# Reordering the small tasks ahead of the FFN in a one-core S4-convolution and SwiGLU kernel: the gate row's parts and the first weights' split

## The chip, the cores and the metric

The kernel runs on one core of a Trainium2 chip. The core has five engines that run side by side, each with its own queue of instructions that it works off in order: TensorE (PE, matrix products into PSUM; its weight loads are listed as PEld), VectorE (DVE), ScalarE (ACT), GpSimd (POOL) and SyncE (SP, which here only starts transfers). An engine waits for another by a semaphore; while the instruction at the head of a queue waits, everything behind it in that queue waits too. The metric is the device time of one execution in microseconds (us), the median of several runs.

## The reference: what is computed

Six rows of 448 numbers come from the condition `c`: `mod = silu(c) @ w_mod`, cut into `sa, ca, ga, sb, cb, gb`. Then two blocks work on `x` (2048 tokens by 448 channels, float32):

```python
h = layernorm(x) * (1 + ca) + sa
x = x + ga * S4(h)            # a long convolution over the tokens, plus h * Dskip
h = layernorm(x) * (1 + cb) + sb
x = x + gb * ((silu(h @ w_gate) * (h @ w_up)) @ w_down)     # 448 -> 1792 -> 448
```

With these inputs the convolution's kernel is nearly linear in time over the whole length, so that the program replaces the Fourier transforms by running sums of tokens (triangular and ramp matrices on TensorE). A flag, worked out on the chip, chooses between this short path and a general one; the short one runs here.

## The kernel before, in words

The 2048 tokens are 16 tiles of 128, and these are worked through in six blocks of 2, 2, 3, 3, 3 and 3 tiles. For each block the FFN runs over 14 slices `f` of 128 hidden channels: `gate_up(f)` (22 matmuls, line 724) makes gate and up, ScalarE and VectorE form `silu(gate) * up` and split it into a high part `phi` and a low part `plo` (lines 739, 752, 755, 756), and `down(f - 1)` (line 768) multiplies the slice before by `w_down`. Weights and activations are each held as a high part and the rest, so that three products of reduced precision stand for one of full precision; "split" below means this. The weights of slices 0 to 2 (gate and up) and 0 and 1 (down) are split ahead of the FFN, the others inside the first block, one slice at a time.

Before the FFN lies a stage that serves the first two tiles. It is a list of small tasks, `PLAN` (lines 43 to 45 hold its end), and its order is written by hand: the tasks are issued in this order, so that each engine's queue gets its share of the list in the list's order. Nothing reorders them later. The tasks that matter here:

| task | engine and line | what it does |
|---|---|---|
| `sp` | PE 248, 251 | the four parts of row `sb`, each on its own 32 partitions of a PSUM bank |
| `spc` | ACT 469 | copies them to SBUF as `qts` |
| `sbt`, `sbc` | PE 373, 376; DVE 379 | turn them and sum the parts: `sb` as columns, `sbc` |
| `gq`, `gqc` | PE 248, 251; ACT 469 | the same parts and copy (`qtb`) for the gate row `gb`; the weights lie in tile `m` |
| `gbk`, `gb` | PE 382; ACT 455 | spread the gate row over 128 partitions, copy it to SBUF |
| `n1q`, `rq`, `xnq` | DVE 437; POOL 167, 168; ACT 490 | layernorm of tile q (0 or 1): product, root (the power, line 168), scaling |
| `trq` | PE 373, 376 | turns tile q to channels on partitions |
| `hiq`, `loq` | ACT 428, four; DVE 433, four | add `sbc` and split into `hhi` and `hlo`, which the FFN reads |
| `l1` | PE 405 | sum over the first tiles for the running sum |
| `lr0`, `lr1` | ACT 413; DVE 410 and a small transfer in ACT's queue, 411 | put the running sums in place |
| `x0` | ACT 455 | copies tile 0's new `x` |
| `w0`, `w01`, `w02` | ACT 123; DVE 125, 127 | split of gate and up weights 0; `w1...` and `w2...` likewise |
| `d00`, `d01` | ACT 115; DVE 117 | split of down weights 0; `d10`, `d11` likewise |
| `fl` | DVE 447, 448 | the flag, which every engine loads at line 506, after the list |

The stage's PSUM tiles come from four banks in turn (`bank()`), in the order in which the tasks are issued. The FFN's first slice reads `hhi` and weights 0 first (its matmuls go over the high parts of all channels before it takes `hlo`), and its two results lie in `DN[2]` and in the next bank; slice 1 uses the two banks after that. SP starts the load of weight slice 3 into the buffer of slice 0 when `w02` has been done.

```python
        for n in names:
            todo[n]()

    rv = nc.values_load(flag[0:1, 0:1], min_val=0, max_val=1)
```

Of the kernel before, what the change touches and what calls it, by code (L numbers as in the profile page):

```python
# [40 lines left out]
ORDER = """sf x0 x1 sc m10 se sd m11 m20 m21 m00 sb m01 sa m40 m41 m30 m31 w0 m50 m51 d0 w1 d1 x2 w2 x3 d2"""  # L41

PLAN = """t4 pa0 t1 S1 t2 pa1 t3 wi ca gp S20 wr ps0 h00 gpc h01 S21 gt a2 gac sq1 ps1 m0 gdm dg t5 k0 S3 h10 cp v00 a3 gdr
m1 k1 cpc gd h11 hd0 v01 ck sq0 v10 hd1 o00 cbw v11 o01 o02 xh1 gc0 sa st0 o10 o12 o13 o14 fs w0 r0 n10 sp xn0 x1 st1 fl r1 n11 gc1 spc
tr0 xn1 sbt w01 sbc gq l1 hi0 tr1 lo0 lr0 w02 hi1 lo1 lr1 gqc x0 gbk gb w1 w11 w12 d00 d01 w2 w21 w22 d10 d11"""
EPS = 1e-5


# [1016 lines left out]
```

## Time and profile before

| what | value |
|---|---|
| three runs | 491.65, 492.12, 492.21 us; median 492.12 us |
| the profiled execution | 490.89 us, of which its span (first to last instruction) 489.1 us |
| TensorE busy in the span | 475.3 us (97%) |
| VectorE, ScalarE, GpSimd busy | 284.2, 155.7, 62.3 us |
| mean granted TensorE clock | 0.992 of full speed |

Times below are microseconds from the start of the span. A row of the timeline gives start, duration, engine, line, operation, the tile written and the tiles read, and the count of instructions merged; a bracket at its end tells how long the engine sat idle before it and what ended that. A row of the windows gives for each engine the busy time and, in brackets, how many instructions it ran, then the granted clock. Ends of matmuls are modelled, so starts are used where they can be.

### The profile page before, as it was taken

To read this page: it belongs to the slowest core of one execution; us is meant where nothing else is said; L and a number is where in the kernel's file an instruction comes from. 1 tells how busy PE (TensorE), PEld (TensorE's weight loads), DVE (VectorE), ACT (ScalarE), POOL (GpSimd) and SP (SyncE) were. 2 spreads that over 40 slices of the span, in tenths; PEclk is the share of its full clock that TensorE was granted. 3 is DMA by queue.
4 is the path that set the end of the run, shared out by engine and by line. 5 is a ranking of instruction groups with operands and counts; after the bars stand their busy time and mean duration, and the time that the engine had idled before them with its cause. 6 is when DMAs were issued, how large, how long until landed. Compare 5 with 4: busy or idle time off the path is not lost.

```text
span 489.1 us, 7021 instructions
## 1 busy us (share of the span) xinstructions
PE 475.3 (97%) x2743; PEld 447.7 (92%) x2743; DVE 284.2 (58%) x549; ACT 155.7 (32%) x336; POOL 62.3 (13%) x83
## 2 busy tenths in 40 slices
PE   8959999999999999999999999999999999999996
PEld 5629988999998999999999999999999999999995
DVE  5866999677885536565554657365475635222225
ACT  6855645432235112232312233231222231211111
POOL 2320000000000041410004031002231000000000
PEclk9998999999999999999999999999999999999999
DMA  8953663020000300001120011130001112000001
GB/s 331 405 187 108 203 199 113 21 95 1 0 2 2 94 1 0 23 27 60 44 92 1 2 43 35 53 102 12 2 0 45 43 44 76 21 1 0 1 1 62
DMA packets 18778, 31.24 MB, mean 64 GB/s; under 512 B 2608, under 2 KB 13488, under 8 KB 18736
## 3 DMA queue, kind: packets, MB, share of 16 engines
q1 hardware_dynamic: 18000, 30.52, 18.3%
q8 instruction: 23, 0.38, 0.3%
q10 hardware_dynamic: 736, 0.19, 0.2%
q14 instruction: 19, 0.16, 0.1%
HBM read 24.61 MB, written 6.03 MB: 63 GB/s over the span
## 4 chain that ended last, share of the span: by engine, by line
PE 88%; DVE 2%; ACT 2%; issue 1%; ACTq 0%; DVEq 0%
PE bank L724 58%; PE dn L768 27%; ACT raw L195 1%; PE bank L928 1%; PE cv L927 0%; PE cv L929 0%; DVE raw L193 0%; PE dn L724 0%; PE bank L206 0%; PE bank L941 0%; PE bank L382 0%; DVE x L807 0%; ACT raw L194 0%; PE cv L942 0%; PE cv L940 0%
## 5 line engine op out<-in xcount | busy, mean ns | idle before, releaser
L724 PE MATMUL bank<-hhi,gu 128*128 128x384 f32 (+1 forms) x1169 | 212.3, 320 | 0.0
L724 PEld LDWEIGHTS bank<-hhi,gu 128*128 128x128 f32 x1169 | 192.1, 189 | 3.5 <-issue 1.1
L724 PE MATMUL bank<-hlo,gu 128*128 128x384 f32 (+1 forms) x668 | 131.9, 319 | 0.0
L724 PEld LDWEIGHTS bank<-hlo,gu 128*128 128x128 f32 x668 | 110.2, 188 | 0.0
L752 DVE TENSOR_TENSOR bank<-raw,bank 128x384 f32<-128x384 f32 (+1 forms) x69 | 36.8, 534 | 125.4 <-PE bank L724 123.0
L755 ACT CAST phi<-bank 128x384 fp32r<-128x384 f32 (+1 forms) x83 | 36.8, 444 | 144.3 <-DVE bank L752 144.3
L739 ACT ACTIVATE raw<-bank 128x384 f32<-128x384 f32 (+1 forms) x70 | 32.8, 469 | 123.1 <-PE bank L724 114.9
L756 DVE TENSOR_TENSOR plo<-bank,phi 128x384 fp32r<-128x384 f32 (+1 forms) x83 | 42.4, 511 | 37.5 <-ACT phi L755 37.5
L768 PE MATMUL dn<-wdh,phi 128*128 128x448 f32 x218 | 58.0, 367 | 0.0
L768 PE MATMUL dn<-wdh,plo 128*128 128x448 f32 x218 | 57.8, 366 | 0.0
L768 PE MATMUL dn<-wdl,phi 128*128 128x448 f32 x218 | 57.6, 366 | 0.0
L768 PEld LDWEIGHTS dn<-wdl,phi 128*128 128x128 f32 x218 | 41.0, 188 | 3.4
L768 PEld LDWEIGHTS dn<-wdh,plo 128*128 128x128 f32 x218 | 41.0, 188 | 3.3
L768 PEld LDWEIGHTS dn<-wdh,phi 128*128 128x128 f32 x218 | 38.8, 188 | 2.0 <-ACT run L951 0.7
L167 POOL TENSOR_SCALAR rsb<-mvb 128x1 f32<-128x1 f32 (+2 forms) x13 | 4.6, 354 | 172.1 <-DVE mvb L151 170.4
L167 POOL TENSOR_SCALAR rsa<-mva 128x3 f32<-128x3 f32 (+1 forms) x6 | 2.2, 360 | 123.3 <-DVE mva L151 123.3
L125 DVE TENSOR_TENSOR gu<-raw,gu 128x768 fp32r<-128x768 f32 x14 | 13.3, 951 | 4.7 <-ACT gu L123 4.7
L123 ACT CAST gu<-raw 128x1024 fp32r<-128x1024 f32 x14 | 14.6, 1046 | 0.0
L902 POOL TENSOR_TENSOR m<-m,gm 128x448 f32<-128x448 f32 x9 | 10.4, 1154 | 21.4 <-DVE m L184 17.5
L916 DVE TENSOR_TENSOR vl<-m,vh 128x448 fp32r<-128x448 f32 x12 | 9.1, 756 | 6.7 <-ACT vh L915 6.1
L117 DVE TENSOR_TENSOR wdl<-rawd,wdh 128x448 fp32r<-128x448 f32 x16 | 9.9, 620 | 3.4 <-ACT wdh L115 3.2
L194 ACT ACTIVATE raw<-raw,rsb 128x64 f32<-128x64 f32 x14 | 4.8, 346 | 21.0 <-DVE raw L193 11.9
(232 smaller groups left out, 420.8 us busy)
## 6 DMA issues: line engine op xcount, KB each, us to landing
raw<-in_B_w_gate_up_dram SPq DMA_DIRECT2D x14, 512.0 KB, 3.8
rawd<-in_B_w_down_dram SPq DMA_DIRECT2D x16, 224.0 KB, 3.9
x<-in_A_u_dram SPq DMA_DIRECT2D x12, 224.0 KB, 2.9
out_dram<-x SPq DMA_DIRECT2D x11, 224.0 KB, 1.9
xd<-raw SPq DMA_DIRECT2D x9, 256.0 KB, 2.0
raw<-xd SPq DMA_DIRECT2D x36, 64.0 KB, 2.0
wm<-in_w_mod_groups_dram SPq DMA_DIRECT2D x5, 448.0 KB, 8.2
wm<-in_w_mod_groups_dram SPq DMA_DIRECT2D x5, 336.0 KB, 8.2
```

What stands on the lines that cost most here:

```text
L117: ve.tensor_tensor(lo, wdn[j], f32(hi), op=OP.subtract)
L123: sc.copy(wgu[j][:, :, 0:4, :], w)
L125: en.tensor_tensor(lo, w[:, :, 0:3, :], f32(hi), op=OP.subtract)
L167: po.tensor_scalar(rs[:, 0:n], self.mv[:, 0:n, 1], EPS, None, op0=OP.add)
L724: pe.matmul(ps[s][:, 0:n], w[:, s, a], (hlo if lo else hhi)[:, k, 0:n], start=first and q == 0, stop=end and q == len(ka) - 1)
L739: sc.activation(p[:, 0:n], ps[0][:, 0:n], AF.Silu)
L752: ve.tensor_tensor(ps[1][:, 0:n], p[:, 0:n], ps[1][:, 0:n], op=OP.mult)
L755: sc.copy(hi[:, 0:n], ps[1][:, 0:n])
L756: ve.tensor_tensor(lo[:, 0:n], ps[1][:, 0:n], f32(hi[:, 0:n]), op=OP.subtract)
L768: pe.matmul(dn[q][:, 0:D], u[:, cs], v, start=f == 0 and z == 0, stop=f == (NF - 3 if last else NF - 1) and z == 2)
L902: (ve if on_v else po).tensor_tensor(v, h, g, op=OP.mult)
L916: ve.tensor_tensor(vl, v0, f32(vh), op=OP.subtract)
```

## The change

Only the order in `PLAN` changes; no task is added or dropped. In the list, `gq` moves from behind `sbc` to ahead of `r1`, `fl` goes behind `r1`, `gqc` goes from behind `lr1` to directly behind `tr0`, `xn1` moves behind `sbt`, `w01` behind `sbc`, and `gbk`, `w02`, `gb`, `lr0` and `x0` change places among the rest.

```diff
-m1 k1 cpc gd h11 hd0 v01 ck sq0 v10 hd1 o00 cbw v11 o01 o02 xh1 gc0 sa st0 o10 o12 o13 o14 fs w0 r0 n10 sp xn0 x1 st1 fl r1 n11 gc1 spc
-tr0 xn1 sbt w01 sbc gq l1 hi0 tr1 lo0 lr0 w02 hi1 lo1 lr1 gqc x0 gbk gb w1 w11 w12 d00 d01 w2 w21 w22 d10 d11"""
+m1 k1 cpc gd h11 hd0 v01 ck sq0 v10 hd1 o00 cbw v11 o01 o02 xh1 gc0 sa st0 o10 o12 o13 o14 fs w0 r0 n10 sp xn0 x1 st1 gq r1 fl n11 gc1 spc
+tr0 gqc sbt xn1 sbc w01 l1 tr1 gbk hi0 w02 lo0 hi1 lo1 gb lr0 x0 lr1 w1 w11 w12 d00 d01 w2 w21 w22 d10 d11"""
```

Written out by queue, this is the end of the list on each engine:

| queue | before | after |
|---|---|---|
| PE | `sp tr0 sbt gq l1 tr1 gbk` | `sp gq tr0 sbt l1 tr1 gbk` |
| ACT | `gc1 spc xn1 hi0 lr0 hi1 [lr1] gqc x0 gb w1` | `gc1 spc gqc xn1 hi0 hi1 gb lr0 x0 [lr1] w1` |
| DVE | `n11 w01 sbc lo0 w02 lo1 lr1 w11` | `n11 sbc w01 w02 lo0 lo1 lr1 w11` |
| POOL | `r1` | `r1` (issued ahead of `fl`) |

`[lr1]` is the small transfer of line 411. SP's own transfers keep their order. `gq` and `tr0` exchange their PSUM banks.

## The prediction

> **What bounds the kernel now.** I read the page first: TensorE fills the span, so only a stage in which TensorE stands still can give time back. The windows, cut where TensorE starts and stops, find that stage.
>
> ```profile
> PE 475.3 (97%) x2743; PEld 447.7 (92%) x2743; DVE 284.2 (58%) x549; ACT 155.7 (32%) x336; POOL 62.3 (13%) x83
> ...
> 31.85:36.74 4.89, 0.00 (x0) 0.00 (x0) 3.30 (x10) 2.30 (x8) 0.00 (x0) 0.77 0.29 105
> ...
> 45.10:97.50 52.40, 51.96 (x351) 47.22 (x351) 45.67 (x87) 27.40 (x53) 2.69 (x4) 1.00 0.44 139
> ```
>
> The first column pair is TensorE. It runs nothing for 4.89 us just ahead of the FFN, and the granted clock falls to 0.50 there; from 45.10 on it is full. The waits say for whom it stood, and the chain, in order of time, what stood before that:
>
> ```profile
> PE bank L382 <- ACT qtb L469: 4.9, 1, 4.9
> ...
> 35.51 0.61 ACTq L411
> ...
> 36.16 0.54 ACT qtb L469
> ...
> 36.74 1.86 PE bank L382 x2
> 38.60 0.21 PE dn L724
> ```
>
> `gbk` (382) waits for the copy `gqc` (469), which stands in ACT's queue behind the transfer of `lr1` (411); the FFN stands behind `gbk`. The timelines of the four engines give all that the sum needs (start, duration, at the end the wait). PE, where 26.40 to 27.00 is `sp`, 27.29 `tr0`, 28.14 `sbt`, 28.98 `gq`, 29.87 `l1`, 30.93 `tr1`, 45.10 `down(0)`:
>
> ```profile
> 26.40 0.57 PE L248 MATMUL bank<-wm,cs 128*32 128x448 f32 x2
> ...
> 27.00 0.35 PE L251 MATMUL bank<-wm,cs 128*32 128x224 f32 x1
> 27.29 0.55 PE L373 MATMUL bank<-ident,h 128*128 128x128 f32 x3
> 28.14 0.55 PE L373 MATMUL bank<-ident,qts 128*128 128x128 f32 x3
> 28.98 0.58 PE L248 MATMUL bank<-m,cs 128*32 128x448 f32 x3
> 29.87 0.68 PE L405 MATMUL cv<-v,all 128*128 128x448 f32 x2
> 30.93 0.55 PE L373 MATMUL bank<-ident,h 128*128 128x128 f32 x3 [0.37 <-ACT h L490]
> ...
> 45.10 0.67 PE L768 MATMUL dn<-wdh,phi 128*128 128x448 f32 x2
> ```
>
> ACT (`xn1`, `hi0`, `w1`) and DVE (`n11`, `w01`, `sbc`, `lo0`, `w02`, `lr1`, `w11`, and the product of slice 0; `hi1` and `lo1` last like `hi0` and `lo0`):
>
> ```profile
> 30.20 0.67 ACT L490 ACTIVATE h<-h,rsb 128x448 f32<-128x448 f32 x1 [2.21 <-POOL rsb L168]
> 30.78 1.12 ACT L428 ACTIVATE hhi<-bank,sbc 128x128 fp32r<-128x128 f32 x4
> ...
> 39.07 1.05 ACT L123 CAST gu<-raw 128x1024 fp32r<-128x1024 f32 x1
> ...
> 28.20 0.66 DVE L437 SCALAR_TENSOR_TENSOR h<-x,mvb,cbw 128x448 f32<-128x448 f32 x1
> 28.80 0.94 DVE L125 TENSOR_TENSOR gu<-raw,gu 128x768 fp32r<-128x768 f32 x1
> 29.67 0.15 DVE L379 TENSOR_REDUCE sbc<-bank 128x4 f32<-128x16 f32 x1
> 31.93 1.12 DVE L433 SCALAR_TENSOR_TENSOR hlo<-bank,sbc,hhi 128x128 fp32r<-128x128 f32 x4 [2.11 <-ACT hhi L428]
> 33.07 0.42 DVE L127 TENSOR_TENSOR gu<-raw,gu 64x256 fp32r<-64x256 f32 x1
> ...
> 34.80 0.63 DVE L410 TENSOR_TENSOR run<-run,dn 32x448 f32<-32x448 f32 x1
> 40.15 0.96 DVE L125 TENSOR_TENSOR gu<-raw,gu 128x768 fp32r<-128x768 f32 x1 [4.72 <-ACT gu L123]
> 44.22 0.43 DVE L752 TENSOR_TENSOR bank<-p,bank 128x256 f32<-128x256 f32 x1
> ```
>
> **The change, part by part.** No instruction is added or dropped; each part is a place in a queue.
>
> *`gq` ahead of `tr0` and `sbt` on PE.* `gq` holds PE from 28.98 to 29.87, 0.89 us, and `sp`, of the same shape, from 26.40 to 27.29, also 0.89. So `gq` runs 27.29 to 28.18, `tr0` (0.85 to the next start) to 29.03, `sbt` (0.84) to 29.87. Both are 0.89 later. If the two groups of parts overlap in the array, this is less; the starts of `sp`'s own matmuls spread over only 0.60 (26.40 to 27.00), which is the lower bound. I take 0.89, as both rows agree.
>
> *`gqc` ahead of `xn1` on ACT.* It can start at 28.2 and takes 0.54, so it ends near 28.8, while `xn1` waits for POOL anyhow; were that cover gone, it would delay `xn1` and `hi0` behind it by 0.54. `gbk` then finds its input ready and follows `tr1` at once.
>
> *`w01` behind `sbc` on DVE, and the root on POOL.* The power of `r1` took three times what that of `r0` took:
>
> ```profile
> 25.82 0.57 POOL L168 TENSOR_TENSOR rsb<-rsb,mhalf 128x1 f32<-128x1 f32 x1
> 28.46 1.71 POOL L168 TENSOR_TENSOR rsb<-rsb,mhalf 128x1 f32<-128x1 f32 x1
> 48.06 1.28 POOL L168 TENSOR_TENSOR rsa<-rsa,mhalf 128x2 f32<-128x2 f32 x1
> ...
> 47.82 0.95 DVE L125 TENSOR_TENSOR gu<-raw,gu 128x768 fp32r<-128x768 f32 x1
> ```
>
> The slow one ends at 30.17, 0.43 after DVE's `w01` (28.80 + 0.94 = 29.74); the one at 48.06 ends 0.57 after the like operation (48.77). So POOL seems held until DVE's operation ends. With `w01` gone, only `n11` (to 28.86) stands in its way: the power ends at 29.3 to 29.45, and `xn1` starts at 29.45 rather than 30.20. The other end is no gain: 30.20 as before. I take 29.45, for both slow rows speak for it. The Trainium skill, page "SBUF — State Buffer", section "Who interferes with whom", says that a VectorE instruction with two SBUF inputs contends with a GpSimd instruction that reads SBUF, and that the second fully blocks until the first is done; the three rows agree, and by that rule too `n11`, which reads `x` and `cbw`, would be the last to block.
>
> *The chain that follows.* `sbc` starts 0.06 after `sbt` (as `tr1` at 30.93 follows `xn1`'s end at 30.87) and ends at 30.08. `w01` follows, 0.87 to the next start, then `w02`, 0.44: to 31.40. On ACT `xn1` yields at 30.03 (0.58), `hi0` waits for `sbc` and runs 30.13 to 31.25. `tr1` starts when `xn1` has ended (30.1) and `l1` is out, between 30.2 and 30.55 (29.87 + 0.68), and takes 0.85 as `tr0` does, so `hi1` starts between 31.27 (1.14 after `hi0`) and 31.5 and ends by 32.65. On DVE `lo0` is due at 31.40, behind `w02` rather than behind `hi0`; `lo1` 1.14 later (31.93 to 33.07), at 32.54; `lr1` at 33.68, ends 34.31. Thus DVE runs without a gap from `sbc` to `lr1`, and this is the path. ACT's transfer comes 0.08 later (35.43 to 35.51), holds 0.61 and 0.04, and `w1` starts at 35.04 instead of 39.07. `gb`, `lr0` and `x0`, about 0.5 each, run on ACT from 32.65 to 34.1 while it would wait for `lr1`: no cost; without that cover they would add 1.5 to `w1`.
>
> *What the FFN gets.* Its first matmul needs `hi1` (32.4 to 32.65) and `gbk`. `gbk` is out of PE at most 0.93 after `tr1` (half of the 1.86 that it cost at half clock), so by 32.4: off the path. The load of the flag and the branch lie in PE's queue behind `gbk`:
>
> ```profile
> 46.59 2.61 PE bank L724 x22
> ```
>
> By the chain no more than 1.86 went by for `gbk`, load and branch together (36.74 to 38.60), at half clock; from 31.4 that is 33.3 at the latest. Slice 0 starts near 32.6, 6 us earlier, and its 22 matmuls take 2.61 at full clock: PE is out at 35.2, or at 35.9 if the branch comes late. But slice 1 needs weights 1, split by `w1` and `w11`. These start 4.03 earlier, not 6: `w11` (1.08 behind `w1`, 39.07 to 40.15) ends at 35.04 + 1.08 + 0.96 = 37.08. PE stands about 1.9 us, slice 1 ends at 39.7, and `down(0)` needs `phi`. From `w1` (39.07) to `down(0)` (45.10) lay 6.03 us, and DVE was busy without a break between `w11` and the product at 44.22; nothing there is reordered. So `down(0)` starts at 35.04 + 6.03 = 41.07 instead of 45.10: **4.0 us** earlier. PE stands another 1.4 us ahead of it; that part of the old wait moves here and is no gain.
>
> *SP.* The load of weights 3 is released by `w02`, now at 31.4, and the next ones, released by `w12` and `w22`, come 4.0 earlier with them. After 41.07 all engines do what they did, shifted; PE was busy for 51.96 of 52.40 us up to 97.50, so the gain stays.
>
> *Sum.* 490.89 - 4.0 = 486.9 for the profiled execution; the median of the runs is 492.12, 1.23 above it, so 488.1. Ends of the terms: `gq` at 0.6 gives 0.3 more (487.8), the power unchanged 0.55 less (below).
>
> **The rivals.** *The power stays at 1.71.* Then `xn1` at 30.20, `hi0` from 30.78, `hi1` from 31.92 to 33.06, `lo1` from 33.09, `lr1` from 34.23, `w1` at 35.59: a gain of 3.48, time 488.6. Against it speak the two slow rows.
>
> *The clock falls in the new gaps.*
>
> ```profile
> 7.25:10.66 3.41, 2.65 (x8) 1.13 (x6) 3.38 (x5) 1.51 (x8) 2.40 (x2) 1.00 1.03 415
> 31.13:34.54 3.41, 0.71 (x7) 0.30 (x5) 2.44 (x9) 2.43 (x8) 0.00 (x0) 1.00 0.00 0
> 34.54:37.95 3.41, 1.21 (x3) 0.80 (x3) 0.86 (x2) 0.97 (x2) 0.00 (x0) 0.50 0.44 155
> 37.95:41.37 3.42, 3.42 (x15) 3.01 (x15) 1.19 (x2) 2.73 (x4) 0.00 (x0) 0.50 0.00 0
> ```
>
> The clock fell at 34.54 and rose at 41.37, twice 3.41 us apart, so I cut windows so. After 0.71 us busy of 3.41 it fell, after 2.65 it did not. Between slices 0 and 1 there will be windows with some 1.5 busy: nearer to the one that fell. If it falls there, slice 1 (22 x 0.21 = 4.6 at half clock, the 0.21 from the chain) begins at 37.1 and would end at 41.7, 0.6 late; over one window most of that hides in the 1.4 of slack (0 to 0.4); over two, as seen, `down(0)` and what follows to 43.9 lose another 1.1. Worst case 1.7: 489.8. The Trainium skill, "TensorE: Matmul & The Clock Gate", section "What's actually happening", halves the clock after an idle window of about 3.4 us; here a window with 21% busy did it. Read strictly, no gap of 1.9 us would, and the sum stays.
>
> *The gain is hidden anyway:* `down(0)` hangs on a transfer rather than on the split, and the time stays 492.1. Weights 1 and 2 were issued by 20.99:
>
> ```profile
> 20.99 0.33 SPq L105 DMA_DIRECT2D raw<-in_B_w_gate_up_dram  x1
> DMA to landing us min/median/max: 3.7/8.6/9.1
> ```
>
> Nothing in the change moves them. They land by 30.1, 5 us before `w1` would want them. Little speaks for it.
>
> *Slower:* `gq`, now right behind `sp` on PE, waits for its weights `m`, with `tr0` and `sbt` behind it.
>
> ```profile
> L280 SPq DMA_DIRECT2D m<-in_w_mod_groups_dram x2: 327/327/327, 15.0 to 15.9; - x2
> DMA to landing us min/median/max: 8.3/8.4/8.4
> ```
>
> They landed at 24.3, 3.0 us ahead of 27.29. Every microsecond past 27.3 costs one; past 31.3 the gain is gone, past 32.3 it is slower by over 0.2%: 493.1 or more. It would take a landing 8 us late.
>
> **How the numbers follow.** The forecast 0.78; power unchanged 0.07; clock 0.08; hidden 0.04; slower 0.03. Predicted is 488.1. The range holds the forecast with its ends and the scatter of runs shown (0.5) below, 487.2, and above it the power's 488.6 and part of the clock's, 489.5. A measurement of this kernel tells about 0.2%, 1.0 us, from no change: faster 0.92, same 0.05, slower 0.03.
>
> **What would show it.** Right: `gqc` before `xn1`; the power near 0.9 with its end near 29.4; no DVE gap from `sbc` to `lr1`; `w1` at 35.1; the first FFN matmul near 32.6 at clock 1.00; waits of 1.9 and 1.4 us on PE ahead of slice 1 and `down(0)`; `down(0)` at 41.1. Wrong: a PE wait at line 248 for `m`; a power of 1.7; clock 0.50 after 36; or a new PE idle stretch behind 45 that gives back the 4 us.

## The result, and the profile after

The changed kernel takes 487.87 us in the median (487.63 to 489.08), the kernel before 492.16 beside it: a ratio of 0.992, interval 0.9901 to 0.9938. That is 4.3 us less, against 4.0 forecast. The profiled execution took 489.08 us, against 486.9 forecast for it; most of that difference is a late start, shown below.

The waits of TensorE in the stage ahead of the FFN, engine and line, for whom, total, count and longest, and the windows cut at TensorE's stops, both of the changed kernel:

```profile
PE bank L724 <- ACT gu L123: 1.4, 1, 1.4
PE bank L724 <- DVE gu L125: 0.6, 1, 0.6
...
33.04:36.66 3.62, 3.62 (x26) 3.05 (x24) 3.17 (x10) 2.76 (x8) 0.00 (x0) 1.00 0.47 145
36.66:39.05 2.39, 0.39 (x3) 0.19 (x2) 0.99 (x2) 2.10 (x3) 0.00 (x0) 1.00 0.01 2
39.05:42.98 3.93, 3.92 (x21) 3.62 (x21) 3.38 (x7) 1.53 (x5) 0.00 (x0) 0.65 0.54 149
47.19:97.00 49.81, 49.39 (x334) 44.64 (x333) 42.54 (x80) 25.55 (x49) 1.21 (x3) 1.00 0.41 131
```

The wait of 4.9 at line 382 is gone. TensorE runs `gbk` and slice 0 in one piece and then stands twice for the split of weights 1, together 2.0 us. The chain, in order of time, now runs through VectorE, then ACT's transfer and `w1`:

```profile
31.43 0.39 PE bank L376 x4
...
31.93 0.17 DVE sbc L379
32.10 0.88 DVE gu L125
...
33.00 0.35 DVE gu L127
...
33.45 1.90 DVE hlo L433 x7
...
35.64 0.64 DVE run L410
...
36.30 0.61 ACTq L411
...
36.95 1.05 ACT gu L123
...
38.03 0.97 DVE gu L125
...
39.05 3.92 PE bank L724 x21
...
42.98 1.76 PE dn L768 x6
```

All this lies some 2 us later on the page than forecast, for a reason ahead of the changed tasks. TensorE's row for the flag's sum, which starts together with `sp`, stands at 28.38 (before: 26.39), because it waited longer for the weights of the six rows, by the waits of the two executions from the start:

```profile
PE bank L238 <- DMA wm<-in_w_mod_groups_dram: 1.0, 2, 0.9
```

```profile
PE bank L238 <- DMA wm<-in_w_mod_groups_dram: 3.2, 2, 1.9
```

(first before, then after.) Nothing in the order up to `sp` differs, and `sp` starts at other times in the experiments below too: 27.63 with the old order and some extra matmuls behind it, 26.96 in a second execution of the changed kernel. So I compare executions from `sp` on, and, at the other end, up to VectorE's last sum (line 807), behind which only the last stores lie. By that measure the kernel before took 458.14 and the changed one 454.18: 3.96 less. The span shows only 1.8 of it; of the other 2.2, 2.0 is the late start.

### The profile page after: what moved, and what is told of

Read it like the earlier page. It is cut to its first block, busy times and chain, and to the rows that moved or that the text cites. A ratio compares the mean times of both kernels' runs of the same rounds, so it can differ in the third digit from the quotient of the medians.

```text
span 487.3 us, 7022 instructions
## 1 busy us (share of the span) xinstructions
PE 474.4 (97%) x2743; PEld 447.1 (92%) x2743; DVE 284.7 (58%) x549; ACT 155.9 (32%) x336; POOL 60.8 (12%) x83
## 3 DMA queue, kind: packets, MB, share of 16 engines
HBM read 24.61 MB, written 6.03 MB: 63 GB/s over the span
## 4 chain that ended last, share of the span: by engine, by line
PE 90%; DMA 3%; DVE 3%; ACT 2%; issue 1%; SPq 0%; ACTq 0%; DVEq 0%
PE bank L724 57%; PE dn L768 27%; DMA wm<-in_w_mod_groups_dram 2%; DMA x<-in_A_u_dram 1%; ACT raw L195 1%; PE dn L454 1%; PE bank L238 1%; PE bank L928 1%; PE cv L927 0%; DVE gu L125 0%; PE cv L929 0%; ACT gu L123 0%; DVE raw L193 0%; PE bank L206 0%; DVE hlo L433 0%
## 5 line engine op out<-in xcount | busy, mean ns | idle before, releaser
L756 DVE TENSOR_TENSOR plo<-bank,phi 128x384 fp32r<-128x384 f32 (+1 forms) x83 | 42.5, 512 | 37.5 <-ACT phi L755 37.5
L768 PEld LDWEIGHTS dn<-wdh,plo 128*128 128x128 f32 x218 | 40.9, 188 | 3.3
```

The source lines that it names most:

```text
L756: ve.tensor_tensor(lo[:, 0:n], ps[1][:, 0:n], f32(hi[:, 0:n]), op=OP.subtract)
L768: pe.matmul(dn[q][:, 0:D], u[:, cs], v, start=f == 0 and z == 0, stop=f == (NF - 3 if last else NF - 1) and z == 2)
```

## The experiments

Each row gives one profiled execution, its times counted from `sp`; "to the last sum" is the measure just named. The last two columns are the median of the timed runs and the ratio to the kernel before.

| kernel | power of `r1` | `w1` starts | `down(0)` starts | to the last sum | median | ratio (interval) |
|---|---|---|---|---|---|---|
| before | 1.71 | 12.68 | 18.71 | 458.14 | 492.16 | 1 |
| changed | 0.84 | 8.57 | 14.60 | 454.18 | 487.87 | 0.992 (0.9901 to 0.9938) |
| changed, once more | 0.83 | 8.57 | 14.69 | 454.03 | 487.93 | 0.9908 (0.9884 to 0.9932) |
| gate row alone | 1.71 | 10.20 | 16.23 | 455.61 | 489.93 | 0.996 (0.9946 to 0.9974) |
| split alone | 0.84 | 11.46 | 17.48 | 456.85 | 490.87 | 0.9976 (0.9965 to 0.9987) |
| before, filled | 1.71 | 11.85 | 17.88 | 457.28 | 491.25 | 0.998 (0.9965 to 0.9995) |
| `w01` back | 1.71 | 9.15 | 15.17 | 454.61 | 489.23 | 0.9955 (0.9936 to 0.9974) |
| changed, filled | 0.84 | 8.58 | 14.61 | 454.16 | 488.72 | 0.9913 (0.9885 to 0.9941) |
| transfer on SP | 0.84 | 7.36 | 13.39 | 452.82 | 486.56 | 0.9885 (0.9855 to 0.9915) |
| transfer on SP, `w1` first | 0.84 | 6.50 | 12.96 | 452.31 | 486.07 | 0.987 (0.9848 to 0.9893) |

The kernel before, run beside them, took 491.93 in the comparison with the gate row alone, the split alone, "before, filled" and "`w01` back", and 492.69 in that with the other four experiments.

Two differences within the table hold nearly everywhere. In eight of its ten rows `down(0)` starts 6.02 or 6.03 behind `w1` (6.12 in the second execution of the changed kernel, 6.46 in the last row, where VectorE reaches `w11` later than ACT would let it), and in all ten it is 439.34 to 439.58 from there to the last sum. So what moves `w1` moves the end.

The theory is the prediction's: what sets the time is when weights 1 are split, at the end of a path through `sbc`, VectorE, ACT's transfer and `w1`. Its strongest rival, which the prediction did not weigh as a cause of the gain, is the clock: before, TensorE ran at half clock from 34.5 to 41.4, which is at most 3.4 us of TensorE's time. TensorE was busy for only 4.63 of these 6.83 us (1.21 and 3.42 in the windows of the prediction), so that 2.3 is the most that it can have cost.

**The changed kernel once more.**

> The changed kernel once more, beside the others: 487.9. If the 2 us by which its first profiled execution started the small tasks late were the order's doing, sp starts near 28.4 again; if it was the loads' doing in that execution, sp may start near 26.4.

`sp` starts at 26.96 here, and from `sp` on all is as in the first execution (`w1` 8.57 in both): the late start was the loads' doing, and the span, 485.7, shows the gain that the first one hid.

**The gate row alone.**

```diff
-... x1 st1 fl r1 n11 gc1 spc tr0 xn1 sbt w01 sbc gq l1 hi0 tr1 lo0 lr0 w02 hi1 lo1 lr1 gqc x0 gbk gb w1
+... x1 st1 gq fl r1 n11 gc1 spc tr0 gqc xn1 sbt w01 sbc l1 hi0 tr1 gbk lo0 lr0 w02 hi1 lo1 gb lr1 x0 w1
```

> Only the gate row's tasks (gq, gqc, gbk, gb) move forward in the order of the kernel before; w01 stays ahead of sbc, w02 behind lo0. Theory (the path is DVE from lo0 to lr1, then ACT's transfer, then w1): the power of r1 stays at 1.7, xn1 at 30.2, lr1 at 34.8 as before, w1 behind transfer and x0 at 36.6 instead of 39.07: 2.45 faster, 489.7. Rival (the gain is the clock alone: TensorE no longer stands long enough to fall to half): nearly the whole gain, 488.0 to 488.5, as the wait for gbk is gone here too.

`w1` came 2.48 earlier (12.68 to 10.20) and the last sum 2.53; the median is 2.0 below the kernel before in the same comparison. TensorE no longer waits for `gbk`, yet it waits behind slice 0 (the timeline of TensorE, second matmul group of slice 1 at 40.22):

```profile
39.23 0.38 PE L724 MATMUL bank<-hhi,gu 128*128 128x256 f32 x1 [1.84 <-ACT gu L123]
40.22 1.65 PE L724 MATMUL bank<-hhi,gu 128*128 128x256 f32 x6 [0.61 <-DVE gu L125]
```

So removing the wait of 4.9 at line 382 is worth 2.5 and not its length: the split of weights 1 decides, as the theory has it. On the clock this run decides nothing. The rival supposed that the clock would stay up here; it fell behind slice 0, and the window from there to `down(0)` has a mean clock of 0.66:

```profile
39.20:44.16 4.96, 4.32 (x22) 4.07 (x22) 4.37 (x8) 2.56 (x6) 0.00 (x0) 0.66 0.44 117
```

**The split alone.**

```diff
-... tr0 xn1 sbt w01 sbc gq l1 hi0 tr1 lo0 lr0 w02 hi1 lo1 lr1 gqc x0 gbk gb w1
+... tr0 sbt xn1 sbc w01 gq l1 hi0 tr1 w02 lo0 hi1 lo1 lr0 lr1 gqc x0 gbk gb w1
```

> Only the order of the weights' split and of tile 1's work moves (xn1 behind sbt, w01 behind sbc, w02 ahead of lo0); gq, gqc, gbk and gb stay late, behind lr1. Theory: the power of r1 falls to some 0.85, xn1 at 29.4, lr1 near 33.6, w1 near 37.9 instead of 39.07: 1.2 faster, 491.0, with the clock still at 0.50 when gbk runs. Rival (clock alone): TensorE still stands for over 4 us ahead of gbk and the clock falls: no gain, 492.2.

`w1` came 1.22 earlier, the last sum 1.29. TensorE still stood 4.3 us for `qtb`, and its clock still fell to 0.50, at 36.8 in that execution. The two halves give 2.53 + 1.29 = 3.8 of 4.0: they add up nearly.

**The clock by itself.** 20 matmuls of 512 columns (`tri` by `tri`, into a bank that is free then), whose results nobody reads, in the wait of the kernel before. The helper `fill`, which issues them, is left out here:

```diff
+            "fill": lambda: fill(DN[2], 20),
-... hi0 tr1 lo0 lr0 w02 ...
+... hi0 tr1 fill lo0 lr0 w02 ...
```

> The kernel before with 20 extra matmuls (tri by tri, results unused) on TensorE in the wait ahead of gbk, so that the clock stays up; nothing else moves. Theory: gbk takes 0.75 instead of 1.86, gb and w1 come 1.1 earlier, the first slice's matmuls at full clock end earlier but wait for the split of weights 1: 1.1 faster, 491.1. Rival (clock alone): the 3.4 us that TensorE lost at half clock come back, 488.8.

The windows of this run (the fill, `gbk`, then the FFN's first two slices up to `down(0)`), and TensorE's row of `gbk` (line 387 there is 382):

```profile
33.02:38.00 4.98, 4.83 (x23) 3.68 (x21) 3.30 (x10) 2.39 (x8) 0.00 (x0) 1.00 0.32 105
38.00:38.97 0.97, 0.97 (x4) 0.53 (x4) 0.00 (x0) 0.38 (x1) 0.00 (x0) 1.00 0.03 4
38.97:45.50 6.53, 5.36 (x45) 5.10 (x43) 4.36 (x8) 4.06 (x8) 0.00 (x0) 1.00 0.32 84
```

```profile
37.99 1.02 PE L387 MATMUL bank<-qtb,pick 128*128 128x448 f32 x2 [0.15 <-ACT qtb L474]
```

The clock is 1.00 throughout, and the gain is 0.83 at `w1` and 0.86 at the last sum, not 3.4 and not 2.3. In the last window TensorE now stands 1.2 of 6.5 us: what slices 0 and 1 save at full clock they wait for `phi` instead. Only `gbk` paid, 1.02 against 1.86 before. That is 0.84, and I had counted 1.1, because I set the spacing of two matmuls where `gb` waits for their end. So the clock is refuted as the cause of the whole gain: cured alone, it is worth 0.86 of the 4.0, and that only because `gbk` stood in the path to `w1`.

**`w01` ahead of `sbc` again.**

```diff
-... tr0 gqc sbt xn1 sbc w01 l1 tr1 gbk ...
+... tr0 gqc w01 sbt xn1 sbc l1 tr1 gbk ...
```

> The changed kernel with w01 back ahead of sbt, sbc on VectorE; the rest as changed. Theory (GpSimd is held while VectorE reads two operands from SBUF): the power of r1 takes 1.7 again and xn1, hi0, lo0 and w1 come 0.5 later: 488.4. Rival (the power's length has another cause): it stays at 0.84, w01 runs while VectorE would idle, and the time is 487.7 to 487.9.

POOL's second power (of `r1`) in the changed kernel, and in this one with VectorE's rows around it (`n11`, `w01`):

```profile
30.45 0.84 POOL L168 TENSOR_TENSOR rsb<-rsb,mhalf 128x1 f32<-128x1 f32 x1
```

```profile
29.83 1.71 POOL L168 TENSOR_TENSOR rsb<-rsb,mhalf 128x1 f32<-128x1 f32 x1
...
29.57 0.67 DVE L437 SCALAR_TENSOR_TENSOR h<-x,mvb,cbw 128x448 f32<-128x448 f32 x1
30.16 0.94 DVE L125 TENSOR_TENSOR gu<-raw,gu 128x768 fp32r<-128x768 f32 x1
```

The power is back at 1.71 and ends at 31.54, again 0.44 behind `w01`; in the changed kernel it ends 0.43 behind `n11` (30.20 + 0.66 to 31.29). `w1` came 0.58 later than in the changed kernel, the last sum 0.43 to 0.58; the prediction's rival of an unchanged power had 0.55. The median, 489.23, is 0.8 above the 488.4 expected; the profiled execution does not show where that comes from, and it stays open.

The Trainium skill's rule ("SBUF — State Buffer", "Who interferes with whom"), as the prediction tells it, is borne out: nothing but the place of one VectorE operation with two SBUF inputs moved, and the power ended behind it. By the rows the power starts ahead of `w01`, but inside `n11` (29.57 to 30.24), which has two SBUF inputs as well; `w01` followed without a gap, and the power ended behind both. The changed kernel holds the counterpart. `n10` is the same operation as `n11`, but its first input (`dn`) lies in PSUM, and the power of `r0` beside it takes 0.57, as short as any power of the kernel before:

```profile
27.53 0.69 DVE L437 SCALAR_TENSOR_TENSOR h<-dn,mvb,cbw 128x448 f32<-128x448 f32 x1
27.81 0.57 POOL L168 TENSOR_TENSOR rsb<-rsb,mhalf 128x1 f32<-128x1 f32 x1
```

**The clock in the changed kernel.** In the first profile of the changed kernel the clock did fall, at 40.2, in the second at 37.5, each time for 3.4 us; with `w01` back, and in the two versions below, it did not in this stage. Six more matmuls between slices 0 and 1 keep it up:

```diff
             for f in range(NF):
+                if fresh and f == 1:
+                    fill(DN[0], 6)
```

> The changed kernel with 6 extra matmuls on TensorE between slice 0 and slice 1, results unused, so that the wait does not let the clock fall. Theory: the half clock from slice 1 on cost the profiled execution only about 0.3 behind down(0); with the clock at 1.00 throughout the time is 487.6, 0.0 to 0.3 faster. Rival (the fall costs as much as the 3.4 us at half rate suggest, 1.7): 486.2.

TensorE's timeline of slice 1 and the start of `down(0)`, first of the changed kernel's second execution (clock 0.50 from 37.5 to 40.9), then with the fill (clock 1.00; line 729 there is 724, 773 is 768, 760 is 755):

```profile
37.62 1.65 PE L724 MATMUL bank<-hhi,gu 128*128 128x256 f32 x6 [0.61 <-DVE gu L125]
39.07 1.05 PE L724 MATMUL bank<-hlo,gu 128*128 128x256 f32 x4
39.92 1.41 PE L724 MATMUL bank<-hhi,gu 128*128 128x256 f32 x7
41.18 0.63 PE L724 MATMUL bank<-hlo,gu 128*128 128x256 f32 x4
41.65 0.59 PE L768 MATMUL dn<-wdh,phi 128*128 128x448 f32 x2
```

```profile
38.03 0.98 PE L729 MATMUL bank<-hhi,gu 128*128 128x256 f32 x6 [0.60 <-DVE gu L125]
38.85 0.64 PE L729 MATMUL bank<-hlo,gu 128*128 128x256 f32 x4
39.32 0.99 PE L729 MATMUL bank<-hhi,gu 128*128 128x256 f32 x7
40.15 0.63 PE L729 MATMUL bank<-hlo,gu 128*128 128x256 f32 x4
41.97 0.47 PE L773 MATMUL dn<-wdh,phi 128*128 128x448 f32 x1 [1.18 <-ACT phi L760]
```

From the first of these rows to `down(0)` it is 4.03 at half clock and 3.94 at full: the half clock ate the 1.18 that slice 1 would have stood for `phi`, and cost 0.1. The last sum agrees, 454.16 with the fill and 454.03 without. The median with the fill, 488.72, misses the 487.6 expected and is 0.8 above the changed kernel's. The profiled one of its runs lost 1.8 in the last store, which landed in 4.2 us instead of 2.4, behind all that differs; whether the others did too is open. The ratios to the kernel before, 0.9913 and 0.9908, do not tell the two apart.

**The transfer on SP's queue.** In the changed kernel `w1` stands behind the transfer of `lr1` in ACT's queue. Here it is issued by SP.

```diff
                 ve.tensor_tensor(run0[e], run1[e], os[1][e], op=OP.add)
-                sc.dma_start(run[0:1], run[127:128])
+                sy.dma_start(run[0:1], run[127:128])
```

> The changed kernel with the transfer of lr1 (line 411) issued from SP's queue instead of ACT's. Theory (behind sbc and lo the path goes through ACT's queue, where w1 stands behind the transfer, which waits for DVE): w1 starts right behind x0, 1.1 earlier against sp's start, w11 1.1 earlier, and so down(0): 486.8. Rival (TensorE's clock or the weights' loads set the start of slice 1): 487.9, as SP's load of weights 3 now waits for lr1 but nothing is gained.

ACT's rows of `x0` and `w1` in this run:

```profile
34.19 0.53 ACT L455 COPY x<-dn 128x448 f32<-128x448 f32 x1
34.62 1.05 ACT L123 CAST gu<-raw 128x1024 fp32r<-128x1024 f32 x1
```

`w1` follows `x0` at once and comes 1.21 earlier (8.57 to 7.36), `down(0)` too, the last sum 1.21 to 1.36: the queue's order was the bound, as the theory says.

**The best version.** On top of that, `lr0` and `w1` come first on ACT:

```diff
-... hi1 lo1 gb lr0 x0 lr1 w1 w11 ...
+... hi1 lr0 lo1 w1 gb x0 lr1 w11 ...
```

> As the one with the transfer on SP, and lr0 directly behind hi1, w1 ahead of gb and x0. Theory: w1's cast runs while VectorE is at lo1, w11 follows lr1 at once, 1.76 earlier than in the changed kernel; slice 1 then starts some 0.5 behind slice 0 and the clock does not fall: down(0) 1.8 earlier, 486.0, 1.3% under the kernel before. Rival: gb, now behind w1, holds the bank that slice 1 needs, and the gain is under 1: 487 or more.

VectorE's rows `lo0` with `lo1`, `lr1`, `w11`, and TensorE's first rows of slice 1 behind its stop and of `down(0)`:

```profile
32.21 2.16 DVE L433 SCALAR_TENSOR_TENSOR hlo<-bank,sbc,hhi 128x128 fp32r<-128x128 f32 x8
34.40 0.63 DVE L410 TENSOR_TENSOR run<-run,dn 32x448 f32<-32x448 f32 x1
35.05 0.96 DVE L125 TENSOR_TENSOR gu<-raw,gu 128x768 fp32r<-128x768 f32 x1
...
36.07 0.97 PE L724 MATMUL bank<-hhi,gu 128*128 128x256 f32 x6 [0.54 <-DVE gu L125]
...
40.09 0.67 PE L768 MATMUL dn<-wdh,phi 128*128 128x448 f32 x2 [1.27 <-ACT phi L755]
```

`w11` follows `lr1` at once, 1.73 earlier against `sp` than in the changed kernel (9.65 to 7.92). One stop of 0.54 is left ahead of slice 1, and TensorE stands 1.27 for `phi` ahead of `down(0)`. At 486.07 it beats both kernels; against the changed one, 487.93 beside it, that is 1.9.

## Why the prediction was right

- *The sum.* `down(0)` was forecast 4.03 earlier; it is 4.11 (18.71 to 14.60 from `sp`), and 4.02 in the second execution. That the median came within 0.2 of 488.1 is in part luck: the medians differ by 4.3 where the traces show 3.96, and the start of one execution alone moves by up to 2.0.
- *`gq` ahead of `tr0` and `sbt`.* `sbc` was to start 3.54 behind `sp` and did at 3.55. Inside it two errors cancelled: `sp` to `tr0` took 1.66 rather than 1.79, as the two groups of parts overlap a little, and `sbc` followed `sbt` by 0.20 rather than 0.06.
- *The power.* Forecast end 29.3 to 29.45, measured 29.30 once the late start of 1.99 is taken off. `w01_back` shows the reason.
- *No VectorE gap from `sbc` to `lr1`; `w1`.* Both so; `w1` at 34.96 with the late start taken off, forecast 35.04.
- *The FFN's first matmul.* Forecast 32.6, behind the whole of `hi1`. It was 33.68, which is 31.69 without the late start: it did not wait for all eight `hi` operations, the last of which ends at 34.31. That term was wrong by 0.9 and cost nothing, because slice 1 waits for the split.
- *The stops.* 2.0 ahead of slice 1, forecast 1.9. The second, 1.4 ahead of `down(0)`, is missing in both profiles, because the rival of the clock came true beside the forecast: in both the clock fell (a clock of 0.50 after 36 stands among the prediction's signs of being wrong) and slice 1 used the slack up. In the 3.41 us ahead of the two falls TensorE was busy for 1.56 and 1.58 us, the "some 1.5" that the prediction itself put nearer to the window that fell; the 0.08 that I gave it did not follow from that. Nor does the strict reading hold here, by which only a wholly idle window halves the clock. What held is the price: over one window it was forecast as 0 to 0.4, and it is 0.1 in one execution and some 0.3 in the other, where `down(0)` too ran partly at half clock (4.21 from `down(0)` to the next, before 3.93).
- *That the gain stays.* From 47.19 to 97.00 TensorE is busy for 49.39 of 49.81 us; from `down(0)` to the last sum lie 439.43 before and 439.58 after.

Of the rivals, the unchanged power, the transfer that hides the gain, and `gq` waiting for `m` did not happen: TensorE shows no wait for `m`.

## What to carry to other kernels

To remove a stop of the busiest engine gains no more than the time by which the next thing that it needs comes earlier: here the first FFN slice came 6 us forward and the kernel gained 4, since the next slice's weights were split behind a small transfer in another engine's queue. Follow the chain one step past the wait that goes, and look at what stands in the same queue ahead of it; moving that transfer to an idle queue was worth another 1.2 us. Before a half clock is blamed, ask whether the matmuls that it slows would have waited anyway.

## What the runs showed that I had not expected

- The start of the small tasks varies by 2 us from one execution to another (`sp` at 26.39 to 28.38), most of it by when the weights of the six rows land (TensorE's wait for them at line 238 is 1.0 to 3.2 us in the ten executions); that is half of the effect studied here, and with the last store's landing (2.4 or 4.2) it would account for most of the scatter between runs, though only the profiled ones were seen.
- The clock fell in the changed kernel with TensorE standing for no more than 1.4 us at a stretch, 2.0 in all; in two executions of the same program it fell at different places, 40.2 and 37.5.
